# Layer 1's second pass: raw weights loaded from ScalarE's queue, low pieces on VectorE, two of the last sums on GpSimd

## The chip, the cores and the metric

The kernel runs on one core of one Trainium2 chip. The metric is device time in microseconds for one execution.

## The reference

Attention with separate softmaxes on q and k, and two dense layers behind it, over 4 x 576 = 2304 tokens of width 512 with an inner width of 2048. All must come out in float32 precision.

```python
def _attn_ref(q, k, v):                      # 4 batches, 8 heads, 576 tokens, width 64
    q_s = softmax(q, axis=-1)                # over the head's width
    k_s = softmax(k, axis=2)                 # over the tokens
    kv = np.einsum('bhsd,bhse->bhde', k_s, v)
    return np.einsum('bhsd,bhde->bhse', q_s, kv)

h = x @ w_in                                 # layer 1: [2304,512] @ [512,2048]
x = (h * sigmoid(h)) @ w_out                 # [2304,2048] @ [2048,512]
h = x @ w_in2                                # layer 2, the same sizes
out = (h * tanh(softplus(h))) @ w_out2
```

[...]

## The kernel before

**Precision.** A matmul takes float32r operands, so every float32 operand is cut into a high piece (its float32r rounding, made by ScalarE) and a low piece (the operand less its high piece, made by a subtraction). Each product is three matmuls per 128 rows: high by high, high by low, low by high.

**Layer 1, first pass and second pass.** The inner width is cut in two halves, and the tokens go through each half in turn. The first pass has six blocks of 384 tokens, the second five blocks: 512, 512, 256, 512 and 512 tokens. For each block and each of a half's eight chunks of 256 inner columns, `ev_g1` (line 752) multiplies the block's tokens `xs` by a chunk of w_in (12 matmuls into one of two PSUM banks), ScalarE takes SiLU of the bank into `gf` and makes the high piece of `g`, and VectorE makes the low piece. Three chunks later `ev_g2` (line 771) multiplies `g` by a chunk of w_out (12 matmuls) into four accumulator banks. At a block's end `ev_e` (line 783) adds the four banks to `xb` on VectorE, and `ev_x` (line 743) makes the two pieces of the next block in the one buffer `xs`: four casts on ScalarE, four subtractions on VectorE. So at a change of blocks TensorE has four products with w_out, then the next block's products with w_in, the third of which needs the first bank back from `gf`.

**Layer 2** runs as a seven-product scheme on 2 x 2 quadrants. Its weights are prepared during layer 1's second pass. A raw tile of 128 x 512 64-bit numbers (512 KB) is loaded into a stage buffer `st`, one of three, by `w_dma` (line 175). `w_take` (line 304) starts the decode: ScalarE turns the upper words into `wt`, VectorE shifts the lower words in place (TENSOR_SCALAR on `st`). `w_join` (line 312) joins the two on VectorE (SCALAR_TENSOR_TENSOR); with it the stage buffer is free. From two decoded tiles a and b, `w_mix` or `o_mix` makes the quadrants' sums on VectorE (four operations of 128 x 256): a third tile m, and a half tile z. Then the pieces: for a, b and m `t_high` (line 352, ScalarE, a cast into a strip of `xa`) and `t_low` (line 358, GpSimd), for z `z_high` (ScalarE) and `z_low` (GpSimd). Seven stores per mix (`put`, SP's queue) take the pieces to the DRAM tiles `wq` and `wo`, which layer 2 reads back. There are 32 tiles, two to a mix, 16 mixes, 112 stores.

**What sets the order.** From the second half of the first pass on every engine runs in the order in which the program is written (class `InOrder`). `w_plan` (line 247) gives each step of the preparation a due time, counted in events (one event is one product of a 512-token block, and a block's start and end count one each; products of smaller blocks count `Q_SHORT` = 0.3). Tile n's take stands at `k + ev*i`, its join one event later, and `ev` is chosen so that the last of the 32 takes' slots ends `Q_END` events before the second product of the last block. At each event the steps that are due are issued, so a take, a mix or a piece stands in an engine's order between the products' own work:

```python
def w_take(n, box):                              # line 304
    while state["dma"] < min(n + 3, len(need)):
        w_dma()                                  # SP: the load of tile n + 2
```

A load waits on its queue until the join three tiles earlier has freed the buffer. Eight completion semaphores (`DMAHW0` to `DMAHW7`) serve all transfers; a transfer also waits for the earlier one on its own semaphore.

**The end.** `sum_g` (line 983) makes four sums of the activated quadrants before their pieces are cut. In the run of layer 2 GpSimd does it; for the last pair of quadrants VectorE does, while TensorE works off the last products of `half`.

Of the kernel before, what the change touches and what calls it, by code (L numbers as in the profile page):

```python
# [7 lines left out]
F32 = mybir.dt.float32  # L8
F32R = mybir.dt.float32r
U32 = mybir.dt.uint32  # L10
ACTF = mybir.ActivationFunctionType
ALU = mybir.AluOpType
# [53 lines left out]
def attention_silu_mish(ctx: ExitStack, tc: tile.TileContext, q, k, v, w_in1, w_out1, w_in2, w_out2, out):  # L66
    nc = tc.nc
    V, S, G, T, SP = (InOrder(tc, e) for e in (nc.vector, nc.scalar, nc.gpsimd, nc.tensor, nc.sync))
# [4 lines left out]
    P = 128  # L73
# [17 lines left out]
    NQ, NS = NCH // 2, NT // (2 * BLK)  # L91
    Q_PAIR, Q_RING, O_RING = 3584, 3, 5
    N_UNIT, G_OWN, HD = 7 * NQ // 2, 10, DM // 2
    Q_END, Q_SHORT = 2.0, 0.3
    SKEW = 3
    TURN = 2

# [76 lines left out]

    def w_dma():
        kind, p, _, c = need[state["dma"]]
        state["dma"] += 1
        L = p // 2
        st = pools["st"].tile([P, 1024], U32, tag="st", name="st")
        if kind == "G1":  # L180
            SP.dma_start(
                st.rearrange("p (k f) -> p k f", k=KC),
                W_IN[L][:, c * 2 * P:(c + 1) * 2 * P].rearrange("(k p) f -> p k f", p=P),
            )
        else:
            SP.dma_start(st, W_OUT[L][c * P:(c + 1) * P, :])
        st_q.append(st)

    nat = {e: i for i, e in enumerate(events)}
# [57 lines left out]
    def w_plan(start):  # L247
# [18 lines left out]
        def when(z):  # L266
            i = max(i for i, v in enumerate(time) if v <= z)
            return i + (z - time[i]) / (time[i + 1] - time[i])
# [5 lines left out]
        for q in range(NQ):  # L274
            n = 2 * N0 + 4 * q
            boxes = [{} for _ in range(4)]
            for i, box in enumerate(boxes):
                plan((when(k + ev * i), w_take, n + i, box), (when(k + ev * i + 1.0), w_join, box))
            for i, mix in ((0, w_mix), (2, o_mix)):
                a, b = boxes[i:i + 2]  # L280
                m, z = {}, {}
                h = k + ev * (i + 1) + 1.3
                plan((when(h), mix, a, b, m, z))
                for j, box in enumerate((a, b, m)):
                    plan((when(h + 0.7 + 0.2 * j), t_high, box), (when(h + 1.1 + 0.2 * j), t_low, box))
                plan((when(h + 1.3), z_high, z), (when(h + 1.7), z_low, z))
                h += 1.9
                if mix is w_mix:
                    for j, box in enumerate((a, b, m)):
                        to = wq[q][:, j * 1024:(j + 1) * 1024]  # L290
                        plan((when(h), put, box, "hi", to[:, :512]), (when(h), put, box, "t", to[:, 512:]))
                    plan((when(h), put, z, "t", wq[q][:, 3072:]))
                else:
                    to = wo[q // 2].rearrange("p (u f n) -> p u f n", u=7, f=2)[:, :, q % 2]
                    for box, at_ in ((a, to[:, 0:5:4]), (b, to[:, 1:6:4]), (m, to[:, 2:4])):
                        plan((when(h), put, box, "hi", at_[:, :, :HD]), (when(h), put, box, "t", at_[:, :, HD:]))
                    plan((when(h), put, z, "t", to[:, 6]))
            k += 4 * ev

    def plan(*steps):  # L300
        for k, f, *args in steps:
            todo.setdefault(int(k), []).append((k, f, *args))

    def w_take(n, box):
        while state["dma"] < min(n + 3, len(need)):
            w_dma()
        box["st"] = st = st_q.pop(0).rearrange("p (n t) -> p t n", t=2)
        box["t"] = t = pools["tm"].tile([P, 512], U32, tag="wt", name="wt")
        S.activation(out=t.bitcast(F32), in_=st[:, 1].bitcast(F32), func=ACTF.Prelu, scale=W_BIAS, alpha=W_SIGN)
        V.tensor_scalar(out=st[:, 0], in0=st[:, 0], scalar1=29, scalar2=None, op0=ALU.logical_shift_right)  # L310

    def w_join(box):
        st, t = box["st"], box["t"]
# [42 lines left out]
        S.copy(box["hi"].bitcast(F32R), box["t"].bitcast(F32))  # L356

    def t_low(box):
        G.tensor_tensor(out=box["t"].bitcast(F32R), in0=box["t"].bitcast(F32), in1=box["hi"], op=ALU.subtract)

    def z_high(z):
        S.copy(z["t"].bitcast(F32R)[:, :HD], z["t"].bitcast(F32)[:, HD:])

    def z_low(z):
        z = two(z["t"])
        G.tensor_tensor(out=z[:, 1].bitcast(F32R), in0=z[:, 1], in1=z[:, 0], op=ALU.subtract)

    def put(box, what, to):
        t = box[what].bitcast(F32)
# [610 lines left out]

    f32s = {}

    def sum_g(k, e, now):

        for n in ("11", "12", "22"):
            settle((k, n), now)
        a11, a12, a21, a22 = (f32s.pop((k, n)) for n in ("11", "12", "21", "22"))
        e.tensor_tensor(out=a22, in0=a21, in1=a22, op=ALU.add)
        e.tensor_tensor(out=a21, in0=a11, in1=a21, op=ALU.subtract)
        e.tensor_tensor(out=a11, in0=a22, in1=a11, op=ALU.subtract)  # L990
        e.tensor_tensor(out=a12, in0=a12, in1=a11, op=ALU.subtract)
        for n, t, d in (("s1", a22, 1), ("s2", a11, 1), ("s3", a21, 2), ("s4", a12, 2)):
            cut(k, n, t, now + d)

    def pair(s, q):
# [32 lines left out]
        for i, (a, m, ps, start) in enumerate(ORDER, 1):  # L1028
# [10 lines left out]
            if i == 6:  # L1039
                act("12", None, now)  # L1040
            if i == SUM_AT and k:
                sum_g(k - 1, G, now)
            if last:
                if i == 6:
                    settle((B11, s + 1), now)
# [123 lines left out]
            at(len(events) + 8 * (s * NQ + q))  # L1169
            pair(s, q)  # L1170
    k = NS * NQ - 1
    sum_g(k, V, 7 * k + 7)
    pend.extend((k // 2, i, f) for i in range(7) for f in range(2))
    for now in range(7 * k + 8, 7 * k + 22):
        background(now, 0.6, 0.6)
# [31 lines left out]
```

## Time and profile before

| | us |
|---|---|
| median of 3 runs | 870.24 (869.85 to 870.64) |
| the profiled execution, device time | 868.75 |
| its span in the profile | 867.0 |
| TensorE (PE) busy, of the span | 832.3 |
| VectorE (DVE) busy | 577.2 |
| ScalarE (ACT) busy | 440.4 |
| GpSimd (POOL) busy | 266.8 |

The second pass of layer 1 begins at about 283 us and ends at about 495 us; what lies before is attention and the first pass, what lies behind is layer 2. A row of a timeline has the start, the time from the start of the first to the end of the last of its instructions, the engine, the operation with output and input, the count, and in brackets how long the engine sat idle before it and what ended that. All lines are L59 or L57, the helper that records each operation, so rows are told apart by their tiles. The profiled execution's device time is 1.75 us above its span, and 1.5 us below the median.

### The profile page before, as it was taken

To read this page: it belongs to the slowest core of one execution; us is meant where nothing else is said; L and a number is where in the kernel's file an instruction comes from. 1 tells how busy PE (TensorE), PEld (TensorE's weight loads), DVE (VectorE), ACT (ScalarE), POOL (GpSimd) and SP (SyncE) were. 2 spreads that over 40 slices of the span, in tenths; PEclk is the share of its full clock that TensorE was granted. 3 is DMA by queue.
4 is the path that set the end of the run, shared out by engine and by line. 5 is a ranking of instruction groups with operands and counts; after the bars stand their busy time and mean duration, and the time that the engine had idled before them with its cause. 6 is when DMAs were issued, how large, how long until landed. Compare 5 with 4: busy or idle time off the path is not lost. (4 is left out here: it accounts for less than half of the span.)

```text
span 867.0 us, 14239 instructions
## 1 busy us (share of the span) xinstructions
PE 832.3 (96%) x5314; PEld 777.1 (90%) x5314; DVE 577.2 (67%) x1025; ACT 440.4 (51%) x874; POOL 266.8 (31%) x261
## 2 busy tenths in 40 slices
PE   7799999999999999959997999999999999999997
PEld 6688988999999887849885899999999999999997
DVE  5898456673266559796997347567865659755556
ACT  5887354564244555646564445445543445544441
POOL 3035111221000016663663023154523426231310
PEclk9999999999999999979998999999999999999999
DMA  9995311220033428997996457676787667886644
GB/s 231 244 239 122 103 37 38 56 55 1 1 95 109 139 96 285 354 317 246 305 351 242 191 195 266 216 289 215 269 299 251 250 239 260 268 302 213 211 128 154
DMA packets 101989, 170.80 MB, mean 197 GB/s; under 512 B 33824, under 2 KB 75808, under 8 KB 98848
## 3 DMA queue, kind: packets, MB, share of 16 engines
q1 hardware_dynamic: 101920, 169.89, 59.9%
q8 instruction: 42, 0.69, 0.3%
q14 instruction: 27, 0.22, 0.1%
HBM read 135.79 MB, written 34.08 MB: 196 GB/s over the span
## 5 line engine op out<-in xcount | busy, mean ns | idle before, releaser
L59 PE MATMUL psum<-x,wall 128*128 128x384 f32 x1008 | 205.3, 339 | 0.0
L59 PE MATMUL psum<-wall,g 128*128 128x256 f32 x1512 | 204.1, 281 | 0.9 <-DVE xb L59 0.9
L59 PEld LDWEIGHTS psum<-wall,g 128*128 128x128 f32 x1512 | 198.5, 189 | 1.1 <-DVE xb L59 1.1
L59 PEld LDWEIGHTS psum<-x,wall 128*128 128x128 f32 x1008 | 172.2, 189 | 1.5 <-DVE x L59 0.7
L59 POOL TENSOR_TENSOR hf<-hf 128x384 f32<-128x384 f32 x92 | 99.2, 1078 | 198.5 <-ACT hf L59 163.7
L59 PE MATMUL psum<-xs,wall 128*128 128x512 f32 (+2 forms) x588 | 128.1, 372 | 17.9 <-ACT gf L59 17.6
L59 PEld LDWEIGHTS psum<-xs,wall 128*128 128x128 f32 x588 | 106.3, 195 | 35.1 <-ACT gf L59 18.6
L59 PE MATMUL psum<-g,wall 128*128 128x512 f32 (+2 forms) x624 | 129.4, 360 | 0.1
L59 PEld LDWEIGHTS psum<-g,wall 128*128 128x128 f32 x624 | 108.9, 188 | 15.2 <-DVE g L59 0.5
L59 POOL TENSOR_TENSOR wt<-wt,xa 128x512 fp32r<-128x512 f32 x48 | 71.6, 1518 | 164.0 <-DVE wt L59 114.6
L59 DVE TENSOR_TENSOR g<-hf,g 128x384 fp32r<-128x384 f32 x168 | 101.9, 638 | 18.4 <-ACT g L59 18.4
L59 DVE TENSOR_TENSOR xb<-psum,xb 128x768 f32<-128x768 f32 (+2 forms) x94 | 80.3, 869 | 47.3 <-PE psum L59 46.9
L57 PE MATMUL psum<-xs,wall 128*128 128x384 f32 x468 | 99.7, 354 | 2.7 <-ACT gf L57 1.8
L59 ACT ACTIVATE hf<-hf 128x384 f32<-128x384 f32 x72 | 37.9, 526 | 102.8 <-DVE hf L59 102.8
L57 PEld LDWEIGHTS psum<-xs,wall 128*128 128x128 f32 x468 | 81.9, 192 | 6.7 <-ACT gf L57 2.7
L57 PE MATMUL psum<-g,wall 128*128 128x384 f32 x432 | 84.9, 343 | 0.0
L59 ACT CAST g<-hf 128x384 fp32r<-128x384 f32 x168 | 79.2, 513 | 5.0 <-DVE hf L59 3.1
L59 DVE TENSOR_TENSOR hf<-psum,sc 128x384 f32<-128x384 f32 x72 | 40.1, 557 | 55.7 <-ACT sc L59 28.2
L57 PEld LDWEIGHTS psum<-g,wall 128*128 128x128 f32 x432 | 74.8, 188 | 1.1 <-DVE g L57 0.2
L59 ACT COPY sc<-psum 128x384 f32<-128x384 f32 x72 | 34.5, 480 | 76.7 <-PE psum L59 76.1
L59 DVE TENSOR_TENSOR g<-gf,g 128x512 fp32r<-128x512 f32 (+2 forms) x49 | 40.4, 826 | 48.6 <-ACT g L59 48.3
L59 ACT ACTIVATE gf<-psum 128x512 f32<-128x512 f32 (+2 forms) x49 | 26.5, 540 | 59.4 <-PE psum L59 56.7
(133 smaller groups left out, 866.6 us busy)
## 6 DMA issues: line engine op xcount, KB each, us to landing
wall<-wq SPq DMA_DIRECT2D x24, 1792.0 KB, 8.1
wall<-wo SPq DMA_DIRECT2D x84, 512.0 KB, 4.2
st<-in_moe_w_in_dram SPq DMA_DIRECT2D x32, 512.0 KB, 5.3
st<-in_moe_w_out_dram SPq DMA_DIRECT2D x32, 512.0 KB, 4.9
wq<-wt SPq DMA_DIRECT2D x32, 256.0 KB, 4.9
wo<-wt SPq DMA_DIRECT2D x32, 256.0 KB, 5.2
wq<-xa SPq DMA_DIRECT2D x24, 256.0 KB, 5.1
wo<-xa SPq DMA_DIRECT2D x24, 256.0 KB, 5.2
```

The costliest lines, as they stand in the source:

```text
L57: return call(*args, **kwargs)
L59: self.last = call(*args, **kwargs)
```

## The change

The loads of layer 2's 32 tiles are issued from ScalarE's queue instead of SP's, each at a due time of its own, three events ahead of the take of the same tile. The low pieces are made by VectorE instead of GpSimd, with wider spacing between pieces, and the stores stand up to 0.9 events later. `Q_END` goes from 2.0 to 3.5, so that `ev` goes from 1.5125 to 1.4656 events. At the end of the kernel VectorE makes two of the four sums and GpSimd the other two, one of them from a result of VectorE in a buffer of its own.

```diff
-    Q_END, Q_SHORT = 2.0, 0.3
+    Q_END, Q_SHORT, Q_LEAD = 3.5, 0.3, 3.0
...
     def w_dma():
         kind, p, _, c = need[state["dma"]]
+        dma = SP if state["dma"] < 2 * N0 else S
...
-            SP.dma_start(st, W_OUT[L][c * P:(c + 1) * P, :])
+            dma.dma_start(st, W_OUT[L][c * P:(c + 1) * P, :])
...
             for i, box in enumerate(boxes):
+                plan((when(k + ev * i - Q_LEAD), w_ahead_to, n + i))
                 plan((when(k + ev * i), w_take, n + i, box), (when(k + ev * i + 1.0), w_join, box))
...
-                    plan((when(h + 0.7 + 0.2 * j), t_high, box), (when(h + 1.1 + 0.2 * j), t_low, box))
-                plan((when(h + 1.3), z_high, z), (when(h + 1.7), z_low, z))
-                h += 1.9
+                    plan((when(h + 1.1 + 0.3 * j), t_high, box), (when(h + 1.8 + 0.3 * j), t_low, box))
+                plan((when(h + 2.0), z_high, z), (when(h + 2.7), z_low, z))
+                h += 2.8
...
     def w_take(n, box):
-        while state["dma"] < min(n + 3, len(need)):
-            w_dma()
+        w_ahead_to(min(n + 2, 2 * N0 - 1) if n < 2 * N0 else n)
...
+    def w_ahead_to(n):
+        while state["dma"] <= n:
+            w_dma()
...
     def t_low(box):
-        G.tensor_tensor(out=box["t"].bitcast(F32R), in0=box["t"].bitcast(F32), in1=box["hi"], op=ALU.subtract)
+        V.tensor_tensor(out=box["t"].bitcast(F32R), in0=box["t"].bitcast(F32), in1=box["hi"], op=ALU.subtract)
...
-        G.tensor_tensor(out=z[:, 1].bitcast(F32R), in0=z[:, 1], in1=z[:, 0], op=ALU.subtract)
+        V.tensor_tensor(out=z[:, 1].bitcast(F32R), in0=z[:, 1], in1=z[:, 0], op=ALU.subtract)
...
-    def sum_g(k, e, now):
+    def sum_g(k, now, end=False):
...
+        e = V if end else G
+        s2 = pools["hf"].tile([P, BLK], F32, tag="hf", name="hf") if end else a11
         e.tensor_tensor(out=a22, in0=a21, in1=a22, op=ALU.add)
-        e.tensor_tensor(out=a21, in0=a11, in1=a21, op=ALU.subtract)
-        e.tensor_tensor(out=a11, in0=a22, in1=a11, op=ALU.subtract)
-        e.tensor_tensor(out=a12, in0=a12, in1=a11, op=ALU.subtract)
+        if end:
+            e.tensor_tensor(out=s2, in0=a22, in1=a11, op=ALU.subtract)
+        G.tensor_tensor(out=a21, in0=a11, in1=a21, op=ALU.subtract)
+        if not end:
+            e.tensor_tensor(out=s2, in0=a22, in1=a11, op=ALU.subtract)
+        G.tensor_tensor(out=a12, in0=a12, in1=s2, op=ALU.subtract)
```

The order on ScalarE at the change from block 0 to block 1, from the last pieces of the first mix to the first `gf` of block 1. Before:

```order
L59 CAST xa<-wt 128x512
L59 CAST wt<-wt 128x256 [waits DVE_49]
L59 ACTIVATE wt<-st 128x512 [waits DMAHW3_49]
L59 ACTIVATE wt<-st 128x512 [waits DMAHW4_49]
L59 CAST xa<-wt 128x512 [waits DVE_49]
L59 CAST xa<-wt 128x512 [waits Activation_49] x2
L59 CAST wt<-wt 128x256 [waits DVE_49]
L59 ACTIVATE wt<-st 128x512 [waits DMAHW5_49]
L59 ACTIVATE gf<-psum 128x512 [waits PE_49]
```

And now:

```order
L59 CAST xa<-wt 128x512
L59 CAST wt<-wt 128x256
L59 DMA st<-in_moe_w_out_dram 128x1024 [waits DMAHW4_49,DVE_49,Activation_49]
L59 ACTIVATE wt<-st 128x512
L59 CAST xa<-wt 128x512 [waits DVE_49]
L59 CAST xa<-wt 128x512
L59 DMA st<-in_moe_w_out_dram 128x1024 [waits DMAHW7_49,DVE_49]
L59 ACTIVATE wt<-st 128x512 [waits DMAHW6_49]
L59 CAST xa<-wt 128x512
L59 CAST wt<-wt 128x256
L59 ACTIVATE gf<-psum 128x512 [waits PE_49]
```

Two loads now stand between the pieces, each with a wait for VectorE (the join that frees its buffer), and `gf` stands behind both.

The order on VectorE at the same place, around the four adds that empty the accumulators. Before:

```order
L59 TENSOR_SCALAR st<-st 128x512 [waits DMAHW3_49]
L59 SCALAR_TENSOR_TENSOR wt<-wt,st 128x512 [waits DVE_49,Activation_49]
L59 TENSOR_TENSOR wt<-wt 128x256
L59 TENSOR_TENSOR wt<-wt 128x256 [waits DVE_49]
L59 TENSOR_TENSOR wt<-wt 128x256
L59 TENSOR_TENSOR wt<-wt 128x256 [waits DVE_49]
L59 TENSOR_TENSOR xb<-psum,xb 128x512 [waits PE_49] x4
L59 TENSOR_SCALAR st<-st 128x512 [waits DMAHW4_49]
L59 SCALAR_TENSOR_TENSOR wt<-wt,st 128x512 [waits DVE_49,Activation_49]
```

And now:

```order
L59 TENSOR_SCALAR st<-st 128x512 [waits DMAHW3_49]
L59 TENSOR_TENSOR wt<-wt,xa 128x512 [waits Activation_49] x3
L59 SCALAR_TENSOR_TENSOR wt<-wt,st 128x512 [waits DVE_49]
L59 TENSOR_TENSOR wt<-wt 128x256 [waits Activation_49]
L59 TENSOR_TENSOR wt<-wt 128x256
L59 TENSOR_TENSOR wt<-wt 128x256 [waits DVE_49]
L59 TENSOR_TENSOR wt<-wt 128x256
L59 TENSOR_TENSOR wt<-wt 128x256 [waits DVE_49]
L59 TENSOR_SCALAR st<-st 128x512 [waits DMAHW4_49]
L59 TENSOR_TENSOR xb<-psum,xb 128x512 [waits PE_49] x4
L59 SCALAR_TENSOR_TENSOR wt<-wt,st 128x512 [waits DVE_49,Activation_49]
```

Three low pieces and one half-size low piece (the fifth of the 128x256 rows) have come in. The last join, behind the adds, is the one that the second of the two loads above waits for.

The order on VectorE at the kernel's end, around the last sums:

```order
 L59 TENSOR_TENSOR xb<-psum,xb 128x768
 L59 TENSOR_TENSOR g_4849<-hf,g_4849 128x384
-L59 TENSOR_TENSOR hf<-hf 128x384 x4
+L59 TENSOR_TENSOR hf<-hf 128x384 x2
 L59 TENSOR_TENSOR g_4848<-hf,g_4848 128x384
 L59 TENSOR_TENSOR xb<-psum,xb 128x768
```

Two of the four sums have left; they stand at the end of GpSimd's order.

## Rows read from the trace of the kernel before

**Rows 1.** Waits of TensorE: engine, line, waited for, us in total, times, longest.

```profile
PE psum L59 <- ACT gf L59: 17.6, 3, 10.1
```

**Rows 2.** VectorE's groups by shape (busy us, mean ns): 240 to 315, then 315 to 470 us.

```profile
L59 DVE SCALAR_TENSOR_TENSOR wt<-wt,st 128x512 uint32<-128x512 uint32 x16 | 11.0, 685 | 0.1
...
L59 DVE TENSOR_SCALAR st<-st 128x512 uint32<-128x512 uint32 x17 | 7.2, 422 | 0.0
...
L59 DVE SCALAR_TENSOR_TENSOR wt<-wt,st 128x512 uint32<-128x512 uint32 x32 | 38.5, 1202 | 1.3
L59 DVE TENSOR_SCALAR st<-st 128x512 uint32<-128x512 uint32 x31 | 26.3, 848 | 0.3 <-DMA st<-in_moe_w_in_dram 0.3
```

**Rows 3.** GpSimd's groups by shape, 315 to 470 us.

```profile
L59 POOL TENSOR_TENSOR wt<-wt,xa 128x512 fp32r<-128x512 f32 x48 | 71.6, 1518 | 164.0 <-DVE wt L59 114.6 <-ACT xa L59 19.1 <-DVE st L59 13.2
```

**Rows 4.** Timeline at the change from block 0 to block 1.

```profile
314.66 11.04 PE L59 MATMUL psum<-g,wall 128*128 128x512 f32 x48
...
317.69 2.49 DVE L59 TENSOR_TENSOR xs<-xa,xs 128x512 fp32r<-128x512 f32 x4
...
320.81 1.56 DVE L59 TENSOR_TENSOR wt<-wt 128x256 f32<-128x256 f32 x4
...
329.47 2.48 DVE L59 TENSOR_TENSOR xb<-psum,xb 128x512 f32<-128x512 f32 x4
...
332.32 5.73 PE L59 MATMUL psum<-xs,wall 128*128 128x512 f32 x24 [1.18 <-ACT gf L59]
```

**Rows 5.** ScalarE's groups by shape, 315 to 470 us.

```profile
L59 ACT CAST xa<-wt 128x512 fp32r<-128x512 f32 x48 | 27.2, 615 | 22.9 <-DVE wt L59 22.9
L59 ACT ACTIVATE wt<-st 128x512 f32<-128x512 f32 x31 | 20.8, 671 | 29.5 <-DMA st<-in_moe_w_in_dram 19.2 <-DMA st<-in_moe_w_out_dram 8.4 <-POOL wt L59 2.0
...
L59 ACT ACTIVATE gf<-psum 128x512 f32<-128x512 f32 x20 | 11.8, 591 | 9.7 <-PE psum L59 9.6
...
L59 ACT CAST wt<-wt 128x256 fp32r<-128x256 f32 x16 | 6.4, 402 | 0.0
```

**Rows 6.** Timeline at the change from block 1 to block 2.

```profile
356.93 2.88 PE L59 MATMUL psum<-xs,wall 128*128 128x512 f32 x12
...
364.47 0.69 ACT L59 ACTIVATE wt<-st 128x512 f32<-128x512 f32 x1 [4.57 <-DMA st<-in_moe_w_in_dram]
...
382.44 0.66 ACT L59 ACTIVATE wt<-st 128x512 f32<-128x512 f32 x1 [5.67 <-DMA st<-in_moe_w_in_dram]
...
385.29 4.81 PE L59 MATMUL psum<-xs,wall 128*128 128x256 f32 x24 [10.13 <-ACT gf L59]
```

**Rows 7.** Timeline at the change from block 3 to block 4.

```profile
439.88 11.04 PE L59 MATMUL psum<-g,wall 128*128 128x512 f32 x48
...
462.64 8.08 PE L59 MATMUL psum<-xs,wall 128*128 128x512 f32 x24 [6.28 <-ACT gf L59]
```

**Rows 8.** Stretches: length, busy us of PE, PEld, DVE, ACT, POOL, PEclk, DMA, GB/s.

```profile
382.00:386.00 4.00, 0.71 (x3) 0.71 (x4) 3.91 (x7) 3.50 (x9) 2.26 (x2) 0.50 1.04 387
...
460.00:464.00 4.00, 1.36 (x3) 1.16 (x4) 1.47 (x4) 3.54 (x7) 2.82 (x3) 0.60 0.35 118
```

**Rows 9.** SP's waits, then the loads (ns to issue, landing in us), 315 to 470 us.

```profile
SPq L59 <- DVE wt L59: 50.2, 16, 9.6
...
L59 SPq DMA_DIRECT2D st<-in_moe_w_in_dram x14: 372/486/895, 320.8 to 436.5; - x14
...
DMA to landing us min/median/max: 3.5/5.2/6.9
```

**Rows 10.** The stretch from block 1's first products to block 2's, columns as in rows 8.

```profile
327.00:371.00 44.00, 42.75 (x188) 34.76 (x187) 38.37 (x52) 25.39 (x49) 28.22 (x21) 1.00 0.94 323
```

**Rows 11.** The kernel's end: timeline, then GpSimd's sums from the page's groups.

```profile
848.56 2.33 DVE L59 TENSOR_TENSOR hf<-hf 128x384 f32<-128x384 f32 x4
...
852.36 11.05 PE L59 MATMUL psum<-wall,g 128*128 128x256 f32 x90 [0.86 <-DVE xb L59]
...
L59 POOL TENSOR_TENSOR hf<-hf 128x384 f32<-128x384 f32 x92 | 99.2, 1078 | 198.5 <-ACT hf L59 163.7
```

More of the change, by code (lines that the diff above doesn't have):

```diff
@@ L180, in w_dma @@
         if kind == "G1":
-            SP.dma_start(
+            dma.dma_start(
                 st.rearrange("p (k f) -> p k f", k=KC),
@@ L987, in sum_g @@
         a11, a12, a21, a22 = (f32s.pop((k, n)) for n in ("11", "12", "21", "22"))
+        e = V if end else G
+        s2 = pools["hf"].tile([P, BLK], F32, tag="hf", name="hf") if end else a11
         e.tensor_tensor(out=a22, in0=a21, in1=a22, op=ALU.add)
-        e.tensor_tensor(out=a21, in0=a11, in1=a21, op=ALU.subtract)
-        e.tensor_tensor(out=a11, in0=a22, in1=a11, op=ALU.subtract)
-        e.tensor_tensor(out=a12, in0=a12, in1=a11, op=ALU.subtract)
-        for n, t, d in (("s1", a22, 1), ("s2", a11, 1), ("s3", a21, 2), ("s4", a12, 2)):
+        if end:
[4 more added lines that the diff above has]
+        G.tensor_tensor(out=a12, in0=a12, in1=s2, op=ALU.subtract)
+        for n, t, d in (("s1", a22, 1), ("s2", s2, 1), ("s3", a21, 2), ("s4", a12, 2)):
             cut(k, n, t, now + d)
@@ L1041, in pair @@
             if i == SUM_AT and k:
-                sum_g(k - 1, G, now)
+                sum_g(k - 1, now)
             if last:
@@ L1171, in attention_silu_mish @@
     k = NS * NQ - 1
-    sum_g(k, V, 7 * k + 7)
+    sum_g(k, 7 * k + 7, True)
     pend.extend((k // 2, i, f) for i in range(7) for f in range(2))
```

## The prediction

> **What bounds the kernel now.** I began with the busy time of the engines in equal stretches, which shows TensorE full almost everywhere except in the second pass of layer 1; the waits of TensorE put the loss there down to one producer, ScalarE's activation gf, with 17.6 us in three waits [rows 1]. The timeline around each of the three shows what held gf up, and the last two kinds of row, operation by operation, what that work costs alone and beside others.
>
> I call the five token blocks of the second pass 0 to 4, and T the moment at which the last product with w_in of a block ends. After T TensorE has four products with w_out left, then the first two of the next block; the third needs a PSUM bank that gf must have emptied. All three waits lie at such block changes. Change 0 to 1: T is 314.66, TensorE runs out at 331.14 and waits 1.18 us [rows 4]. Change 1 to 2: T is about 359.7 (356.93 plus one product, a quarter of the 11.04 us that four take [rows 7]); it runs out at 375.16 and waits 10.13 us [rows 6]. Change 3 to 4: T is 439.88, it runs out at 456.36 and waits 6.28 us [rows 7]. After the two long ones the granted clock is low: 0.50 and 0.60 of full in the stretches where TensorE had been idle, that is partly or wholly 1.2 instead of 2.4 GHz [rows 8]. It costs 8.08 - 5.73 = 2.35 us after change 3 to 4 (24 equal matmuls in rows 7 and 4), and by the same share of 4.81 us some 1.4 us after change 1 to 2. Lost in all: 1.18 + 10.13 + 1.4 + 6.28 + 2.35 = 21.3 us. This is all that the first two edits can win.
>
> Why is gf late? At change 1 to 2 ScalarE sat 4.57 us and later 5.67 us before a decode, waiting for raw weights [rows 6]. A load lands 5.2 us after its issue, and SP issues it behind stores that wait for VectorE 50.2 us in all [rows 9]. At the other two changes VectorE itself is late. It works 38.4 us of 44 [rows 10], and much of that is sharing: a shift takes 0.42 us and a join 0.69 us before GpSimd has work, 0.85 and 1.20 us beside it [rows 2].
>
> **The change, part by part.** Low pieces: GpSimd loses 48 subtractions of 1.52 us [rows 3] and 16 half-size ones. VectorE gains 48 at about 0.62 us (it does the same subtraction on xs, four in 2.49 us [rows 4]) and 16 at 0.39 us (the mix, four in 1.56 us [rows 4]): 36 us. What goes is the sharing: 32 x 0.52 + 31 x 0.43 = 30 us on joins and shifts alone [rows 2], some more on g and xs. So VectorE's load hardly moves; what matters is the order at the block changes, where I walk each chain with the lone durations.
>
> ScalarE's costs, from [rows 5]: decode 0.67, high piece 0.62, half-size piece 0.40, gf 0.59; a load issue 0.49 us, as on SP [rows 9] (nothing in this trace shows an issue on ScalarE; 0 and 0.9, the longest on SP, bound it, and over the issues that stand before gf that is 1 us either way). A stage buffer is one of three, so the load of tile n waits for the join of tile n-3 on VectorE, and now ScalarE waits there, with gf queued behind it.
>
> Change 0 to 1. VectorE ends the xs subtractions at 320.18 [rows 4]. Up to the join that frees the buffer for the load just ahead of gf it then has four joins (2.74), two mixes (3.12), three shifts (1.26), three low pieces (1.86), a half-size one (0.39) and the four adds that empty the accumulators (2.48): 11.8 us, to 332.0. Then on ScalarE issue, decode, piece, half piece, gf: 2.8 us, TensorE resumes at 334.8 instead of 332.32. A second wait follows: the next load also stands ahead of the second gf, and its join comes after a g piece, a low piece and the join (1.9 us) that need the first g: second gf done at 339.1, while TensorE is ready for it at 337.5. Waits of 3.6 + 1.6 = 5.2 us instead of 1.18: **4.0 us lost**.
>
> Change 1 to 2. With the loads no longer behind the stores ScalarE is on time at T. It has gf, g, a decode, two pieces, then four short xs casts, and VectorE the last subtraction: T + 4.8. The same list on VectorE, with one half-size piece more, is 12.2 us, so T + 17.0, and 2.8 us on ScalarE bring gf to T + 19.8 = 379.5 against 385.29: **5.8 us won**. TensorE is out of work at about T + 13.6, so 6 us of waiting and the slow clock after it stay.
>
> Change 3 to 4. The earlier end of the decodes (Q_END 3.5) leaves one load here, ahead of the xs casts, and puts the accumulator adds behind the last mix. ScalarE has gf, g, an issue, a decode, two pieces and four xs casts, VectorE's last subtraction ends at T + 6.2; then three joins, two mixes, a half piece, two shifts, three low pieces: 8.3 us; then three pieces, a half piece, gf: 2.8 us. T + 17.3, where TensorE runs out at T + 16.5: a wait of 0.8 instead of 6.28 us. The 1.18 us wait was followed by 24 matmuls at full pace [rows 4], so the slow clock goes as well: 5.5 + 2.35 = **7.8 us won**.
>
> The end. Before the last products VectorE does four sums in 2.33 us, and TensorE waits 0.86 us for an accumulator add behind them [rows 11]. With two sums moved the add is 1.2 us earlier, and the wait would go. But GpSimd's sums take 1.08 us each [rows 11] and run beside VectorE's. One operation held for the length of one of them gives the gain back. Bounds +0.86 and -0.3; I take **+0.4**, between, since joins beside GpSimd took 0.5 us more on average, not 1.1 [rows 2]. The Trainium skill, "SBUF — State Buffer", section "Who interferes with whom", says that a VectorE operation with two SBUF inputs and a GpSimd one that reads SBUF exclude each other for a whole instruction, whichever starts second. By that rule alone the term is 0; the doubled shifts and joins agree with it.
>
> Other moves cost nothing that I can see. The first 32 loads stay on SP. The stores now wait for VectorE instead of GpSimd, whose three pieces took 4.6 us [rows 3] and now take 1.9, so they leave earlier. GpSimd has nothing else there. Beyond the pass, TensorE is full.
>
> Sum: -4.0 + 5.8 + 7.8 + 0.4 = 10.0 us off the profiled execution's 868.75, which is 1.5 us under the median of the runs: **860.2 us** against 870.24.
>
> **Rivals.**
> (a) The joins come earlier than I walk them and all three waits vanish, and the tail too: 870.2 - 21.3 - 0.9 = 848. For it: VectorE's slow operations were all beside GpSimd. Against it: 11.8 and 12.2 us of work in one engine's fixed order between xs and gf. 0.12.
> (b) The transfers set the pace. The tiles read are 32 of 512 KB and 112 stores of 256 KB are written, 46 MB; one 44 us stretch already runs at 323 GB/s with the DMA engines 0.94 busy [rows 10], and the plan is packed 3% tighter. Then a load lands in 6.9 instead of 5.2 us [rows 9]; twice that at the changes takes 3.4 us of my gain, and up to 8 us if changes 0 to 1 and 1 to 2 each lose a full 4: 864 to 868. Here the Trainium skill speaks against the edit: "DMA: Bandwidth & Descriptors", section "Issuing engines are not separate DMA queues", has all queues on the same 16 engines, so that another issuer saves only issue time. What the trace shows ahead of the loads, though, is SP waiting, which the rule does not cover. 0.18.
> (c) Slower: ScalarE, in whose order gf stands, is held by its own loads. A load also waits for an earlier transfer on its completion semaphore, most often a store of the group before; if that store is late, one landing (5.2 us) falls on gf at change 0 to 1 and another at 1 to 2, and the longer wait at 0 to 1 brings the slow clock (2.35): 860.2 + 10.4 + 2.35 = 873. The point: more than 10 us of added holding. Against it: in my walk such a store has landed before VectorE's join frees the buffer of the load that gf stands behind. 0.13.
> (d) It does not do what it says: VectorE's load is the same, and each wait goes only to the next change: 870 +- 1.7. 0.07.
>
> **Numbers.** Forecast 0.50: 852 to 866, from the issue cost, the tail's bounds and 4 us of error in each walked chain. Range over the cases, leaving out the fast half of (a) and most of (c): 850 to 871. This kernel's runs can tell 0.2%, 1.7 us, from no change. Faster: 0.50 + 0.12 + 0.18 = 0.80; same 0.07; slower 0.13.
>
> **What would show it.** Right: no GpSimd work between 320 and 466 us, joins at 0.69 and shifts at 0.42 us, a wait for gf at block changes 0 to 1 (two pieces, some 5 us) and 1 to 2 (some 6 us), hardly any at 3 to 4, a low clock only after 1 to 2; ScalarE's waits for raw weights gone, and waits for VectorE ahead of its loads instead. Wrong: change 0 to 1 without a wait means that the join is not what holds gf; a wait at 3 to 4 that the earlier end did not help; joins still above 1 us that something else slowed VectorE.

## The result, and the profile after

After: **860.92 us** median of 4 runs (860.07 to 863.23); before, in the same comparison, 870.05 us (868.92 to 870.64). The ratio is 0.9901, 95% interval 0.9879 to 0.9923, that is 6.7 to 10.5 us of 870. The forecast was 860.2 us with a range of 850 to 871.

The profiled execution of after took 863.23 us (span 861.4), the slowest of its four, and that of before 868.75, below its median. So the traces differ by 5.5 us where the medians differ by 9.1. The traces account for 5.3 of the 5.5, as "Why the prediction was right" shows; the rest of the 9.1 stands in no row that I can name.

First the page of after, busy time of each engine (answering to the table of before): GpSimd has lost 85 us, VectorE 11.

```profile
span 861.4 us, 14136 instructions
...
PE 832.6 (97%) x5314; PEld 777.9 (90%) x5314; DVE 566.5 (66%) x1087; ACT 440.9 (51%) x874; POOL 181.5 (21%) x199
```

TensorE's waits, as in [rows 1] (us in total, times, longest): five waits for gf instead of three.

```profile
PE psum L59 <- ACT gf L59: 13.2, 5, 6.9
```

VectorE's groups by shape, 312 to 465 us, as in [rows 2]: joins and shifts at the lone durations of [rows 2], and the 48 low pieces.

```profile
L59 DVE TENSOR_TENSOR wt<-wt,xa 128x512 fp32r<-128x512 f32 x48 | 31.1, 685 | 0.7 <-ACT xa L59 0.6
L59 DVE TENSOR_TENSOR wt<-wt 128x256 f32<-128x256 f32 x64 | 24.2, 420 | 0.6
L59 DVE SCALAR_TENSOR_TENSOR wt<-wt,st 128x512 uint32<-128x512 uint32 x32 | 22.0, 686 | 0.6
...
L59 DVE TENSOR_SCALAR st<-st 128x512 uint32<-128x512 uint32 x32 | 13.5, 422 | 0.0
```

ScalarE's decodes, 312 to 465 us, as in [rows 5]: ScalarE sits idle ahead of them for 40.0 us instead of 29.5, and no longer for raw weights but for VectorE, whose joins free the buffers of the loads that stand there.

```profile
L59 ACT ACTIVATE wt<-st 128x512 f32<-128x512 f32 x32 | 21.5, 673 | 40.0 <-DVE wt L59 20.1 <-DVE st L59 12.5 <-issue 7.1
```

The timeline of after at change 0 to 1, as in [rows 4]. Read from the bottom: TensorE resumes when gf is done; gf stands behind a decode that was idle for 2.91 us, that one behind a load (ACTq) issued at 334.02, and the load behind the join that VectorE starts at 333.30, right after the accumulator adds. The first rows show something that I had not walked: ScalarE was held by a load already at T, so the xs casts started late.

```profile
315.65 11.04 PE L59 MATMUL psum<-g,wall 128*128 128x512 f32 x48
...
318.46 0.35 ACTq L59 DMA_DIRECT2D st<-in_moe_w_out_dram  x1
318.86 0.66 ACT L59 ACTIVATE wt<-st 128x512 f32<-128x512 f32 x1 [1.75 <-DVE st L59]
319.42 2.17 ACT L59 CAST xs<-xa 128x512 fp32r<-128x512 f32 x4
...
330.91 2.48 DVE L59 TENSOR_TENSOR xb<-psum,xb 128x512 f32<-128x512 f32 x4
333.30 0.68 DVE L59 SCALAR_TENSOR_TENSOR wt<-wt,st 128x512 uint32<-128x512 uint32 x1
...
334.02 0.35 ACTq L59 DMA_DIRECT2D st<-in_moe_w_out_dram  x1
...
334.41 0.67 ACT L59 ACTIVATE wt<-st 128x512 f32<-128x512 f32 x1 [2.91 <-DVE st L59]
...
335.79 0.60 ACT L59 ACTIVATE gf<-psum 128x512 f32<-128x512 f32 x1
...
336.44 7.27 PE L59 MATMUL psum<-xs,wall 128*128 128x512 f32 x24 [4.31 <-ACT gf L59]
```

TensorE at the other changes, as in [rows 6, 7]: change 1 to 2 (T is 365.31), a new pair of waits at 2 to 3, and change 3 to 4 (T is 443.02).

```profile
365.31 11.04 PE L59 MATMUL psum<-g,wall 128*128 128x512 f32 x48
...
376.19 3.03 PE L59 MATMUL psum<-xs,wall 128*128 128x256 f32 x24
386.09 5.09 PE L59 MATMUL psum<-xs,wall 128*128 128x256 f32 x24 [6.87 <-ACT gf L59]
...
414.15 3.02 PE L59 MATMUL psum<-xs,wall 128*128 128x512 f32 x12 [0.23 <-ACT gf L59]
418.40 3.02 PE L59 MATMUL psum<-xs,wall 128*128 128x512 f32 x12 [1.23 <-ACT gf L59]
...
460.03 5.73 PE L59 MATMUL psum<-xs,wall 128*128 128x512 f32 x24 [0.53 <-ACT gf L59]
```

The granted clock (the column PEclk, 0.58, 0.50, 0.68 and 1.00) in stretches of after, columns as in [rows 8]: low after both long waits, not only after change 1 to 2, and full after change 3 to 4.

```profile
336.00:340.00 4.00, 3.56 (x10) 2.87 (x11) 2.90 (x6) 1.52 (x3) 0.00 (x0) 0.58 1.04 368
...
384.00:388.00 4.00, 1.91 (x9) 1.91 (x10) 2.28 (x6) 2.85 (x7) 0.00 (x0) 0.50 0.94 340
388.00:392.00 4.00, 4.00 (x26) 4.00 (x26) 1.83 (x4) 1.54 (x4) 0.00 (x0) 0.68 0.80 283
460.00:464.00 4.00, 3.97 (x17) 3.30 (x18) 4.00 (x8) 2.63 (x5) 0.00 (x0) 1.00 0.69 231
```

The kernel's end in after, as in [rows 11]: the wait for the accumulator add is 0.42 us instead of 0.86; GpSimd's two sums take 1.3 us each beside VectorE's.

```profile
843.54 1.14 DVE L59 TENSOR_TENSOR hf<-hf 128x384 f32<-128x384 f32 x2
...
844.23 2.61 POOL L59 TENSOR_TENSOR hf<-hf 128x384 f32<-128x384 f32 x2 [12.31 <-DVE hf L59]
...
846.89 11.05 PE L59 MATMUL psum<-wall,g 128*128 128x256 f32 x90 [0.42 <-DVE xb L59]
```

### The profile page after: what moved, and what is told of

Same layout as the page of the kernel before. It is cut to its first block, busy times and chain, and to the rows that moved or that the text cites. A ratio compares the mean times of both kernels' runs of the same rounds, so it can differ in the third digit from the quotient of the medians.

```text
span 861.4 us, 14136 instructions
## 1 busy us (share of the span) xinstructions
PE 832.6 (97%) x5314; PEld 777.9 (90%) x5314; DVE 566.5 (66%) x1087; ACT 440.9 (51%) x874; POOL 181.5 (21%) x199
## 5 line engine op out<-in xcount | busy, mean ns | idle before, releaser
L59 POOL TENSOR_TENSOR hf<-hf 128x384 f32<-128x384 f32 x94 | 101.8, 1083 | 210.7 <-ACT hf L59 172.4
L59 PE MATMUL psum<-xs,wall 128*128 128x512 f32 (+2 forms) x588 | 127.3, 370 | 13.2 <-ACT gf L59 13.2
L59 DVE TENSOR_TENSOR g<-gf,g 128x512 fp32r<-128x512 f32 (+2 forms) x49 | 30.5, 623 | 52.7 <-ACT g L59 52.4
L59 POOL TENSOR_TENSOR x<-xb,x 128x384 fp32r<-128x384 f32 x5 | 5.1, 1018 | 284.7 <-DMA wall<-wq 279.2
```

The source lines that it names most:

```text
L59: self.last = call(*args, **kwargs)
```

## The experiments

My theory: VectorE is no longer slowed by GpSimd, and what is left is order. gf waits on ScalarE behind a load, which waits for a join, which stands on VectorE behind the work of the block's end. The rivals: the transfers set the pace; the later end (Q_END) or the wider spacing is the gain and the pieces' engine does not matter. The table collects all runs but the one of the kernel's end, which was measured once. The waits for gf are those of one profiled execution, by change of blocks; the times are medians.

The experiments ran in four comparisons, each with runs of before beside it, whose medians lie between 868.12 and 869.26 us; after ran only in the first comparison of all, beside 870.05. A distance between two rows is therefore taken from the ratios as well (0.01 is 8.7 us), and their intervals leave it uncertain by some 3 to 4 us.

| kernel | us | ratio to before (95%) | 0 to 1 | 1 to 2 | 2 to 3 | 3 to 4 |
|---|---|---|---|---|---|---|
| before | 870.05 | 1 | 1.18 | 10.13 | 0 | 6.28 |
| after | 860.92 | 0.9901 (0.9879 to 0.9923) | 4.31 | 6.87 | 1.46 | 0.53 |
| low pieces back on GpSimd | 873.90 | 1.0062 (1.0038 to 1.0086) | 5.79 | 9.89 | 0.86 | 5.51 |
| loads back on SP | 850.55 | 0.9801 (0.9774 to 0.9828) | 2.06 | 2.60 | 0 | 0.53 |
| Q_END 2.0 | 855.61 | 0.9858 (0.9827 to 0.9890) | 2.65 | 2.80 | 0 | 2.39 |
| four stage buffers | 850.43 | 0.9794 (0.9773 to 0.9814) | 1.27 | 3.65 | 0 | 0.54 |
| before, low pieces on VectorE | 861.47 | 0.9896 (0.9864 to 0.9928) | 0 | 9.32 | 0 | 3.62 |
| loads on SP and Q_END 2.0 | 856.98 | 0.9853 (0.9820 to 0.9886) | 0 | 4.14 | 0 | 4.25 |
| the same, paced, Q_LEAD 2.2 | 854.67 | 0.9835 (0.9810 to 0.9860) | 0 | 5.67 | 0 | 0 |
| loads on SP, four stage buffers | 854.24 | 0.9827 (0.9801 to 0.9852) | 0 | 7.00 | 0 | 0.53 |
| old spacing | 856.53 | 0.9854 (0.9826 to 0.9881) | 3.71 | 4.13 | 0 | 0 |
| four buffers, paced, Q_END 2.0 | 848.72 | 0.9755 (0.9716 to 0.9794) | 0 | 3.26 | 0 | 0 |
| the same, old spacing | 846.28 | 0.9737 (0.9715 to 0.9758) | 0 | 1.91 | 0 | 0.33 |

**Low pieces back on GpSimd**, all else as changed.

```diff
-        V.tensor_tensor(out=box["t"].bitcast(F32R), ...
+        G.tensor_tensor(out=box["t"].bitcast(F32R), ...
...
-        V.tensor_tensor(out=z[:, 1].bitcast(F32R), ...
+        G.tensor_tensor(out=z[:, 1].bitcast(F32R), ...
```

> The changed kernel with its low pieces back on GpSimd, all else as changed. Theory (sharing): joins and shifts beside GpSimd go back to about 1.2 and 0.85 us; between the xs subtractions and the join that gf hangs on lie four joins and three shifts, 4 x 0.52 + 3 x 0.43 = 3.4 us more, less 2.25 us of pieces that VectorE no longer makes, so each of the two long waits grows by 1 us or more, and the wait at change 3 to 4 comes back: 865 to 872 us. Rival (the later spacing and Q_END are the whole gain, the engine of the pieces does not matter): 861 +- 1.7 us.

Measured 873.9 us, 13.0 above after (14.0 by the ratios), a little above the theory's range, and slower than before. VectorE's groups, 312 to 465 us, beside those of after above: sharing is back, if not the whole of it.

```profile
L59 DVE SCALAR_TENSOR_TENSOR wt<-wt,st 128x512 uint32<-128x512 uint32 x32 | 32.2, 1006 | 1.1
...
L59 DVE TENSOR_SCALAR st<-st 128x512 uint32<-128x512 uint32 x32 | 24.4, 763 | 0.0
```

The two long waits grew by 1.48 and 3.02 us, and 3 to 4 came back at 5.51 us. On VectorE's way from xs to the adds at change 0 to 1 a join takes 1.64 us, a shift 1.51 and four mixes 3.06 beside GpSimd's pieces, where after has 0.69, 0.42 and 1.55. So the pieces' engine decides, and the other edits without it lose 4.6 us (873.90 against the 869.26 of before in the same comparison). What this run does not tell apart is a second path: 19.9 us of ScalarE's idle time ahead of its decodes are put down to the landing of stores, and SP's stores wait 47.1 us for GpSimd's pieces.

**Loads back on SP**, due at the same places.

```diff
-        dma = SP if state["dma"] < 2 * N0 else S
+        dma = SP
```

> The changed kernel with all loads of layer 2's tiles on SP's queue again, due at the same places. Theory (a queue that waits): loads stand behind stores that wait for VectorE's pieces, ScalarE's waits for raw weights come back at change 1 to 2 (4 us or more there), while gf no longer stands behind a load's wait for the join (change 0 to 1 wins up to 4 us): 861 to 868, most likely 864 us. Rival (the DMA engines' pace decides, the queue does not): no change, 861 +- 1.7 us, and the waits for gf at the same places.

Measured 850.55 us, 10.4 faster than after (8.7 by the ratios): outside both theories. ScalarE's groups here, 312 to 465 us, show that its waits for raw weights did come back, 24.5 us of them, but most lie where they hold no gf.

```profile
L59 ACT ACTIVATE wt<-st 128x512 f32<-128x512 f32 x31 | 20.9, 675 | 24.5 <-DMA st<-in_moe_w_out_dram 13.5 <-DMA st<-in_moe_w_in_dram 10.9
```

The same kernel's timeline at change 1 to 2. The decode ahead of gf did not wait for a join; the one before it waited 2.83 us for its transfer, and gf starts at T + 16.1 (T is 359.68), where in after it starts at 385.67, T + 20.4.

```profile
359.68 11.04 PE L59 MATMUL psum<-g,wall 128*128 128x512 f32 x48
...
372.29 0.69 ACT L59 ACTIVATE wt<-st 128x512 f32<-128x512 f32 x1 [2.83 <-DMA st<-in_moe_w_in_dram]
...
374.39 0.66 ACT L59 ACTIVATE wt<-st 128x512 f32<-128x512 f32 x1
...
375.77 0.37 ACT L59 ACTIVATE gf<-psum 128x256 f32<-128x256 f32 x1
```

It speaks against the transfers as the bound of after as well: between 315 and 470 us a load lands 5.4 us after its issue in after and 6.0 us here (medians), so that slower transfers go with a faster kernel.

**Q_END 2.0**, loads on ScalarE.

```diff
-    Q_END, Q_SHORT, Q_LEAD = 3.5, 0.3, 3.0
+    Q_END, Q_SHORT, Q_LEAD = 2.0, 0.3, 3.0
```

> The changed kernel with Q_END back at 2.0 (ev 1.5125). Theory: the wait at change 3 to 4 comes back, 4 to 6.3 us instead of 0.5, with the slow clock of 2.35 us behind it, and the changes 0 to 1 and 1 to 2 stay within 2 us: 866 to 870 us. Rival (with the sharing gone VectorE is early enough at 3 to 4 by itself): 861 +- 1.7 us.

Measured 855.61 us: 5.3 faster than after (3.7 by the ratios, just clear of nothing), where I expected 5 to 9 slower. The wait at 1 to 2, expected within 2 us of 6.87, is 2.80. TensorE's waits in order of time:

```profile
333.21 7.32 PE L59 MATMUL psum<-xs,wall 128*128 128x512 f32 x24 [2.65 <-ACT gf L59]
...
378.84 4.52 PE L59 MATMUL psum<-xs,wall 128*128 128x256 f32 x24 [2.80 <-ACT gf L59]
...
452.01 5.73 PE L59 MATMUL psum<-xs,wall 128*128 128x512 f32 x24 [2.39 <-ACT gf L59]
```

At 3 to 4 the wait is 2.39 us and the 24 products behind it run at full pace (5.73): Q_END 3.5 buys 1.9 us there and costs 5.7 us of waiting at the first two changes and 1.5 at 2 to 3. Of the 5.75 us that went at 3 to 4 against before, 3.89 went without Q_END. It takes the pieces' move: with the pieces on GpSimd and Q_END 3.5 the wait is 5.51 us, and in the kernel before the move alone brings it to 3.62 (below).

**Four stage buffers**, loads on ScalarE (one buffer fewer for decoded tiles, to make room).

```diff
-("gf", 2), ("st", 3), ("tm", W_WAIT + 2)):
+("gf", 2), ("st", 4), ("tm", W_WAIT + 1)):
```

> The changed kernel with four stage buffers instead of three (and nine instead of ten buffers for decoded tiles, to make room), so that a load waits for the join of tile n-4. Theory (gf is held by the load ahead of it, which waits for a join that stands behind the accumulator adds): the join it waits for is now a tile earlier, ahead of those adds, and gf waits only for the mix: 3 to 4 us off each of the waits of 4.31 and 6.87 us, and part of the low clock: 851 to 857 us. Rival 1 (the pieces ahead of gf, not the load, hold it): 860 to 862. Rival 2 (fewer buffers for decoded tiles, which stores free, hold the decodes): 863 or more.

Measured 850.43 us. The timeline at change 0 to 1: the load ahead of gf is issued at 328.33, before VectorE's adds are through, and needs no join behind them. This is the theory's own test, and it holds, a little beyond its range; by the ratios the buffer gives 9.3 us. (TensorE's row below stops at the end of the stretch that was asked for; its 24 products take 5.76 us.)

```profile
326.65 2.48 DVE L59 TENSOR_TENSOR xb<-psum,xb 128x512 f32<-128x512 f32 x4
328.33 0.35 ACTq L59 DMA_DIRECT2D st<-in_moe_w_out_dram  x1
328.72 0.67 ACT L59 ACTIVATE wt<-st 128x512 f32<-128x512 f32 x1 [1.49 <-DMA wq<-wt]
...
330.11 0.58 ACT L59 ACTIVATE gf<-psum 128x512 f32<-128x512 f32 x1
...
330.75 1.43 PE L59 MATMUL psum<-xs,wall 128*128 128x512 f32 x5 [1.27 <-ACT gf L59]
```

What ScalarE waits for now (1.49 us) is a buffer of decoded tiles, whose store has to land first.

**Before with only the low pieces on VectorE**: the same two lines as in the first experiment, the other way, in the kernel before.

> The kernel before with its low pieces on VectorE and nothing else changed (loads on SP, Q_END 2.0, the old spacing, the old end). Theory (the pieces' engine is the whole gain, the queue and Q_END give part of it back): joins 0.69 and shifts 0.42 us, waits for gf in the second pass of 3 to 8 us in all, 848 to 856 us. Rival 1 (the loads must leave SP, or the spacing must be wider, for the pieces to help): ScalarE waits for raw weights or low pieces at the changes as before, 860 to 870 us.

Measured 861.47 us, 7.1 below the 868.54 of before in its comparison: in the rival's range, and by the ratios the same as after (0.9896 and 0.9901). But the rival held that the pieces need the other edits to help, and they do not: the moved pieces alone give as much as the whole change, with joins at 0.686 and shifts at 0.423 us. What is left is the rival's picture, at change 1 to 2: the decode ahead of gf sits 4.90 us for raw weights whose load stood on SP behind stores.

```profile
379.74 0.67 ACT L59 ACTIVATE wt<-st 128x512 f32<-128x512 f32 x1 [4.90 <-DMA st<-in_moe_w_in_dram]
...
382.59 5.03 PE L59 MATMUL psum<-xs,wall 128*128 128x256 f32 x24 [9.32 <-ACT gf L59]
```

**The end undone**: all four last sums on VectorE, still with the buffer of its own and the new order of the sums, so not wholly as before.

```diff
-        G.tensor_tensor(out=a21, in0=a11, in1=a21, op=ALU.subtract)
+        e.tensor_tensor(out=a21, in0=a11, in1=a21, op=ALU.subtract)
...
-        G.tensor_tensor(out=a12, in0=a12, in1=s2, op=ALU.subtract)
+        e.tensor_tensor(out=a12, in0=a12, in1=s2, op=ALU.subtract)
```

> The changed kernel with all four last sums on VectorE again. Theory: the wait of the last products for the accumulator add is 0.8 to 0.9 us again instead of 0.42, the time 0.4 us longer, which one time cannot show; the row does. Rival (the two sums on GpSimd delay VectorE's as long as they save): 0.42 us stays.

One run, 862.77 us; the rows are what counts.

```profile
842.89 2.08 DVE L59 TENSOR_TENSOR hf<-hf 128x384 f32<-128x384 f32 x4
...
846.37 11.05 PE L59 MATMUL psum<-wall,g 128*128 128x256 f32 x90 [0.54 <-DVE xb L59]
```

Of the 0.44 us that the end won, moving two sums to GpSimd gives 0.12; the other 0.32 came without it. Neither expectation had that. The row repeats well enough to say so: the wait is 0.42 or 0.43 us in all eleven profiles with the changed end, and 0.86 in both with the old one. The four sums take 2.08 us here and 2.33 before; whether the new order or the buffer of its own does that, no run separates.

**Loads on SP and Q_END 2.0**: the second and third diffs together.

> The changed kernel with loads on SP and Q_END 2.0. The loads alone gave 10 us and Q_END alone 5, but both shorten the same waits, of which 5.2 us and a low clock of some 1.5 us stayed with the loads on SP. Theory (at the change of blocks VectorE has too many steps between xs and gf, and a wider ev takes some away): 844 to 849 us. Rival (Q_END only eased what the loads on ScalarE had cost): 850.5 +- 1.7 us.

Measured 856.98 us, outside both: the two gains do not add, together they are worse than the loads alone (by 4.5 us in the ratios) and no better than Q_END alone. At change 1 to 2 a load that stood behind stores is late for the decode ahead of gf (the 24 products behind it take 5.49 us in all; the row stops at the end of the stretch):

```profile
372.98 0.66 ACT L59 ACTIVATE wt<-st 128x512 f32<-128x512 f32 x1 [4.12 <-DMA st<-in_moe_w_in_dram]
...
374.48 1.86 PE L59 MATMUL psum<-xs,wall 128*128 128x256 f32 x7 [4.14 <-ACT gf L59]
```

With Q_END 3.5 the queue is worth 8.7 us by the ratios (10.4 by the medians); with 2.0 it is worth nothing that the runs can tell (0.9858 from ScalarE, 0.9853 from SP; the medians differ by 1.4 us the other way). Either queue holds gf. That the slots of the plan against the block changes decide which of its waits ends last, and that Q_END shifts all of them, is my reading of these rows and not shown by a run of its own.

**A paced plan** on top of that.

```diff
-            time.append(time[-1] + (1.0 if blocks[e[1]][e[2]][1] == 512 else Q_SHORT))
+            time.append(time[-1] + (0.0 if e[0] in "EX" else 0.6 if e[0] == "G2" and e[3] >= NCH - SKEW else 1.0 if blocks[e[1]][e[2]][1] == 512 else Q_SHORT))
```

> As e10 (loads on SP, Q_END 2.0), with the plan's count of time changed: a block's start and end count nothing, the three products with w_out after a block's last chunk 0.6 of an event (there VectorE also makes xs and empties the accumulators), and Q_LEAD 2.2, since ev is shorter. Theory: two tiles fewer stand between xs and the first gf of a block, all waits for gf go (under 1 us in all), 842 to 846 us. Rival (what is taken away at the changes comes back inside the blocks, where ev is shorter): ScalarE or VectorE is late for g or gf elsewhere, 847 us or more.

Measured 854.67 us, not clear of the run before. The waits for gf at 0 to 1, 2 to 3 and 3 to 4 are gone, but at 3 to 4 TensorE waits 1.10 us for xs instead, and 1 to 2 has 5.67 us left: the rival's time, though its wait lies at a change and not inside a block.

**Loads on SP with four stage buffers** (the second and fourth diffs).

> The changed kernel with loads on SP and four stage buffers (nine for decoded tiles). Theory (in either queue a load ahead of gf starts only when a stage buffer is free, and a fourth buffer takes that wait away): with loads on ScalarE the fourth buffer gave 10 us; with loads on SP that wait was off gf's path except where SP stood behind stores, so little is left to win, 848 to 851 us. Rival (the fourth buffer helps by itself, by landing everything a tile earlier): the two gains add, 843 us or less.

Measured 854.24 us, outside both, and behind either part alone (0.9827 against 0.9801 and 0.9794, at the edge of what the intervals tell). A fourth buffer does nothing for a load that stands behind stores; at 1 to 2 the decode waits 4.17 us for one.

```profile
373.73 0.68 ACT L59 ACTIVATE wt<-st 128x512 f32<-128x512 f32 x1 [4.17 <-DMA st<-in_moe_w_in_dram]
```

**Four buffers, paced, Q_END 2.0**, loads on ScalarE (the third, fourth and paced diffs).

> The changed kernel, loads on ScalarE, with four stage buffers (nine for decoded tiles), Q_END 2.0, and the plan's count of time as in the run before (a block's start and end nothing, the three products after a block's last chunk 0.6). Two tiles instead of three or four stand between xs and gf at change 0 to 1, three at change 1 to 2. Theory: waits for gf under 2 us in all and no low clock, 843 to 848 us. Rival (nine buffers for decoded tiles: decodes wait for stores of pieces, the more so where the plan is denser): a wait of 3 us or more at change 1 to 2 stays, 849 us or more.

Measured 848.72 us, between the two. The wait left, at 1 to 2, is the rival's: a decode sits for a buffer of decoded tiles. The 24 products behind it take 4.63 us in all (the row stops at the end of the stretch) instead of 3.03, at a granted clock of 0.50 from 377 to 379 us.

```profile
372.62 0.67 ACT L59 ACTIVATE wt<-st 128x512 f32<-128x512 f32 x1 [2.73 <-DMA wo<-wt]
...
375.74 1.62 PE L59 MATMUL psum<-xs,wall 128*128 128x256 f32 x9 [3.26 <-ACT gf L59]
```

**The old spacing** in the changed kernel.

```diff
-                    plan((when(h + 1.1 + 0.3 * j), t_high, box), (when(h + 1.8 + 0.3 * j), t_low, box))
-                plan((when(h + 2.0), z_high, z), (when(h + 2.7), z_low, z))
-                h += 2.8
+                    plan((when(h + 0.7 + 0.2 * j), t_high, box), (when(h + 1.1 + 0.2 * j), t_low, box))
+                plan((when(h + 1.3), z_high, z), (when(h + 1.7), z_low, z))
+                h += 1.9
```

> The changed kernel with the pieces and stores spaced as before (0.7, 1.1, 1.3, 1.7 and 1.9 events behind the mix). Theory (the load ahead of gf holds it; the pieces around it are 0.6 us each): the same four loads stand between xs and gf at change 0 to 1, the last one right ahead of gf, so that both long waits stay within 2 us of 4.3 and 6.9: 858 to 864 us. Rival (the wider spacing carries the gain, since low pieces on VectorE would else stand in line behind high pieces that are not made): 866 us or more.

Measured 856.53 us, 4.4 faster than after (4.1 by the ratios) and faster than the theory's range; the wait at 1 to 2 fell by 2.7 us, more than it allowed. The wider spacing costs here.

**The best**: the paced kernel with four buffers and the old spacing.

> The run before (four stage buffers, paced plan, Q_END 2.0, loads on ScalarE) with the pieces and stores spaced as in the kernel before. In that run a decode ahead of gf at change 1 to 2 sat 2.73 us for a buffer of decoded tiles whose store had not landed. Theory: stores leave up to 0.9 events (2.6 us) earlier, the buffers come free as much earlier, the wait of 3.26 us goes to under 1 us and no low clock stays: 843 to 846 us. Rival (tighter pieces make ScalarE wait for the mix and the low pieces ahead of gf): the wait stays or grows, 848 us or more.

Measured 846.28 us (845.98 to 848.10), 14.6 below after (14.3 by the ratios). The wait at 1 to 2 went to 1.91 us, not under 1, and the 24 products behind it take 3.13 us, the full pace. TensorE's two waits for gf that are left (a third, of 0.21 us, is for xb):

```profile
374.32 3.13 PE L59 MATMUL psum<-xs,wall 128*128 128x256 f32 x24 [1.91 <-ACT gf L59]
...
444.90 5.74 PE L59 MATMUL psum<-xs,wall 128*128 128x512 f32 x24 [0.33 <-ACT gf L59]
```

## Why the prediction was right

The time and most of the signs were right (a low clock after change 0 to 1 was not among them); the sum was not. By the traces, each change over the stretch that the brackets name:

- **Change 0 to 1: 4.0 us lost in the forecast, 4.7 in the trace** (T to the T of the next block, 44.99 us before and 49.66 after). gf hangs on the load and the join, as walked, and TensorE resumes at T + 20.8 where I had T + 20.1. The second wait is there too, but TensorE does not show it: the 24 products take 7.27 instead of 5.73 us at a low clock, and the second gf falls inside. What I missed is that ScalarE waits for a load ahead of the xs casts too (1.75 us), so that VectorE's last xs subtraction ends at T + 6.9 instead of T + 5.5.
- **Change 1 to 2: 5.8 won in the forecast, 4.6 in the trace** (T to the first product with w_out: 30.29 and 25.71 us). The step that failed is "With the loads no longer behind the stores ScalarE is on time at T", and again a load is the reason: the gf at T waits behind one issued at 366.31, after a join, and starts at T + 1.4; VectorE then makes three low pieces ahead of the xs subtractions, which end at T + 6.9 instead of T + 4.8. TensorE resumes at T + 20.8 where I had T + 19.8 (T + 25.6 before), after a wait of 6.87 us instead of 6: 4.9 won by that. The slow clock behind it costs 5.09 - 3.03 = 2.06 us and cost 4.81 - 3.03 = 1.78 before, not the 1.4 that I had scaled: 0.3 lost.
- **Change 2 to 3: nothing in the forecast, 2.1 us lost.** I did not walk it, since it had no wait before. Its second gf stands behind a load (issued at 416.71) that waits for a join, as at 0 to 1.
- **Change 3 to 4: 7.8 won in the forecast, 8.1 in the trace** (the wait 6.28 to 0.53, the T to resume 22.76 to 17.01, the slow clock gone). Size right, cause half wrong: I gave it to the earlier end, but with Q_END 2.0 the wait is only 2.39 us and no slow clock follows, and with the pieces on GpSimd the earlier end leaves 5.51 us.
- **The end: +0.4 in the forecast, +0.44 in the trace.** Right in size, by luck: only 0.12 of it is GpSimd's doing, and the rest came with the new order and buffer, which I had put at nothing. The Trainium skill, "SBUF — State Buffer", section "Who interferes with whom", would, as I read it in the prediction, have made the term 0. The 0.12 us lies nearer to that than to my 0.4, and the operations do slow each other, though by some 0.05 and 0.2 us each and not by the length of a whole one: VectorE's two sums took 1.14 us where four without GpSimd took 2.08, and GpSimd's 1.3 each where 1.08 is usual [rows 11].

Sum by the trace: -4.7 + 4.6 - 2.1 + 8.1 + 0.4 = 6.3 us, against 10.0 forecast. Ahead of the second pass after was 1.0 us later than before (T is 315.65 and 314.66), which leaves 5.3 of the 5.5 that the traces differ by. That the medians differ by 9.1, near the forecast, is thus partly luck: the trace supports about 6.

Prices. The low piece is 0.685 us instead of 0.62, a load issue on ScalarE 0.35 to 0.39 instead of 0.49; neither matters. "VectorE's load hardly moves" and the lone durations held, and the first experiment shows that the sharing is what the pieces' move buys. The whole gain lies there: 7.1 us alone in the kernel before, 13.0 in the changed one (9.0 and 14.0 by the ratios).

What was wrong behind the right number is "the first two edits" as a common gain. Undone alone, the loads on ScalarE cost 8.7 us by the ratios, Q_END 3.7, the wider spacing 4.1. These are not three costs that add: SP and Q_END 2.0 together give 4.2 back, and the kernel with only the pieces moved, which has none of the three, is no faster than after. What each is worth depends on the others.

The step behind it is a reading of [rows 9]: "SP issues it behind stores that wait for VectorE 50.2 us in all". They are not the stores' waits. In the trace of before the transfer behind each of the 16 is a load, which waits there for the join that frees its buffer; SP's waits for GpSimd's pieces, on which the stores stand, are 12.7 us. The timeline of SP before shows it: from the start of the first of two loads to the end of the second it is 5.03 us, a store takes 0.39.

```profile
365.96 5.03 SPq L59 DMA_DIRECT2D st<-in_moe_w_out_dram  x2
371.08 0.39 SPq L59 DMA_DIRECT2D wo<-xa  x1
```

So the edit did not take the loads away from a wait, it moved the wait for the join into ScalarE's order, ahead of gf (40.0 us of idle time ahead of the decodes instead of 29.5). And with the loads back on SP ScalarE's waits for raw weights stay nearly what they were before (24.5 us against 27.6 in [rows 5]); in front of gf at change 1 to 2 the wait is 2.83 us instead of 5.67.

The rivals. (b), the transfers, as what sets the pace of after: refuted. In the stretch from 320 to 380 us after moves 322 GB/s, the kernel with four buffers 355, and it ends 10 us earlier; with loads on SP they land later, and the kernel is faster. Whether they bound the faster kernels, whose DMA engines are 0.95 to 1.01 busy in that stretch (0.95 in after), is not shown. The Trainium skill ("DMA: Bandwidth & Descriptors", section "Issuing engines are not separate DMA queues") has another issuer save only issue time. An issue took 0.35 to 0.49 us here, but the issuer's place in line was worth 8.7 us of the kernel's time in one plan and nothing clear in another, which the rule does not cover. (c) came in half: the decodes ahead of gf in after end their idle time with VectorE's join, not with a landing, so its completion semaphores play no part; but ScalarE is held by its own loads, at about the 10 us that it named, and the low clock after 0 to 1 came (1.54 us). The pieces' move outweighed it. (a) did not come, every change has a wait, nor did (d): the joins take 0.686 us, and the waits went from 17.6 to 13.2 us in all.

## What to carry to other kernels

A DMA issue in a compute engine's queue waits there for its buffer, and everything behind it waits along; before moving one, find which instruction frees the buffer and what that stands behind, or give it one more buffer (9 to 10 us here). When one edit of several removes the cause of a wait, walk the others against the trace as it will be, not as it was: here one edit alone gave what all gave together, and each of three others, undone alone, made the kernel 4 to 9 us faster. Where background work is spread over a schedule by a count of events, count an event by the room that it leaves on the engine in question; that, Q_END 2.0, a fourth buffer and earlier stores together took the waits for gf from 13.2 to 2.2 us. The fourth buffer's part is clear of noise by itself; the others' parts on top of it are not.

## What the hardware showed that I had not expected

The waits for gf in the second pass nearly give the time: 2.2 us in all with 846 us, 5.2 with 851, 7.8 with 856, 13.2 with 861, 22.1 with 874. That is about 1.4 us of time for each us of waiting, and the spans of all fourteen profiled executions lie within 2.5 us of such a line (with the 1.10 us for xs counted). Part of the 0.4 is the low clock; the rest is not shown. It was not always the longer wait that the low clock followed: in the kernel with loads on SP a wait of 2.06 us at 0 to 1 was followed by 12 products in 4.60 us, one of 2.60 at 1 to 2 by 24 of half the width in 3.13, the full pace, with clocks of 0.50 from 334 to 336 us in the first case.
